# Where an instruction's semaphore waits stand: the last one at the instruction, the others at instructions ahead of it

## The chip, the core and the metric

The kernel runs on one core of a Trainium2 chip. The metric is the time of one execution in device microseconds. Five engines work side by side, each through its own instruction stream in a fixed order: TensorE (PE, matmuls; its weight loads are shown as PEld), VectorE (DVE), ScalarE (ACT), GpSimd (POOL) and SyncE (SP, which here only issues transfers). They meet at semaphores alone: an instruction adds one to a semaphore when it is done, and another engine's instruction waits until the count has reached a number.

## What is computed

Two kinds of layer alternate over a sequence of 2048 rows of 512 columns, twice each. Cut to what matters:

```python
x = x + A(layernorm(x)); x = x + B(layernorm(x))     # and both once more

def A(x):                                # 64 segments of 32 rows, one after the other
    mem = mem0                           # 8 rows
    for s in range(64):
        h = concat(mem, x[32 * s:32 * s + 32])          # 40 rows
        q, k, v = h @ Wq, h @ Wk, h @ Wv                # 32 heads of 128
        p = softmax(where(mask, q @ k.T / sqrt(128), -1e9))
        o = (p @ v) @ Wo
        mem, out[s] = o[:8], o[8:]       # the next segment needs mem

def B(x):                                # linear attention over all rows, 32 heads of 16
    pq, pk = phi(q), phi(k)              # phi(t) = (t + 1 if t > 0 else exp(t)) + 1e-6
    kv, z = pk.T @ v, pk.sum(rows)
    return (pq @ kv / (pq @ z + 1e-6)) @ wo
```

The 8 memory rows make layer A a recurrence: segment s + 1 can't begin its projections before segment s has ended its attention and its output projection, for those 8 rows.

## The kernel before

**The work.** `a_layer` (twice) goes over 64 segments. In each, `project` makes q, k and v from the 40 rows for two halves b = 0 and 1 of the heads (PE at L2159, and L2047 where loaded weights are used again). ACT or DVE move the results out of PSUM (`evac`, recorded at L1927 on ACT and L1928 on DVE), and DVE turns q and k (L2178). Then comes the path of the memory rows, for each half b in `mem_attention`: scores on PE (L2293, L2285), exponentials on ACT (L2300 for the memory rows, L2304 for the others), a product with a mask on DVE (L2308), P times V on PE (`pvm`, L2321), a reciprocal on DVE (L2326), scaling on ACT or DVE (L2336, L2338), a turn on DVE (L2328). `out_block` multiplies with Wo on PE (L2414), ACT takes over one half of the result (L1927) and DVE adds the other (L2425); `next_mem` puts the 8 new memory rows into place for the next segment (PE L2442, then L1927 or L1928). The attention of the 32 other rows (`x_attention`: PE L2364 and L2384, DVE L2352, L2371, L2374, L2391) and the pieces of layer B (`b_in`: L2597, L2668, L2675; `b_out`: L2059, L2831, L2843) aren't on that path; their matmuls stand between those of the path. Rows that are done go by transfers from SP and POOL (L1944) to a buffer, from which DVE adds them to x (L2491).

**The order.** Every operation is a node with a key, the engines that may run it, a planned cost and what it depends on. The order isn't found by the program: the table `PLACE` gives each node a place, a number from 1 to about 13500, and sometimes the engine. `schedule` sorts by it, hands out the 8 PSUM banks in that order and checks that whatever a node depends on stands ahead of it. Each engine gets its own nodes in that order. A node on PE is a group of 4 to 16 matmuls or so.

**The waits.** `finalize` (from L1718) gives each engine a semaphore and each sort of transfer one, and goes through the nodes in order. For a node it collects, for each semaphore, the highest count that the nodes it depends on will have reached, and leaves out what its engine knows already from earlier waits. What is left is `nd.waits`, with the highest count first:

```python
            items = sorted(need.items(), key=lambda kv: -kv[1])
...
            for si, v in items:
                if know[si] < v and infer[si] < v:
                    waits.append((si, v))
```

`emit` calls `wait_ge` (L1770) for each of them, in the order of the list, and then the node's first instruction. In the built program the wait that was called first is part of that instruction; the others stand ahead of it as instructions of their own, which the trace names EVENT_SEMAPHORE and puts at L1770. For a matmul with a weight load it is the load that carries the wait. As DVE's count runs ahead of ACT's, a PE node that waits for both engines has DVE's wait in its own instruction and ACT's in an EVENT_SEMAPHORE ahead of it. Of the 252 nodes at L2321, 159 wait for both: for DVE's product (L2308) and for ACT, which frees PSUM and moves v (L1927).

## Time and profile before

| | |
|---|---|
| median of 3 runs | 1542.52 us (1540.34 to 1544.87) |
| the profiled execution | 1539.86 us, its span 1538.1 us, so 1.8 us lie around the span |
| PE, DVE, ACT, POOL busy | 95%, 82%, 59%, 13% of the span |
| granted TensorE clock | 0.997 on average |

Three views are used below. The **page** gives totals and the chain of work that ended last, followed back from the end. The **timeline** lists instructions in the order of time: start in us, length in us, engine, line, what is written and read, how many were merged, and in brackets how long the engine had been idle before and who ended that. The view of **one source line** gives, for L1770, the semaphore instructions: how many, the shortest, median and longest record in ns, and when the first and the last began. A matmul's end is modelled, so starts are compared, not ends.

### The profile page before, as it was taken

The page shows a single profiled execution, that of the slowest core. Times are in us where ns is not written, and L with a number is a line of the kernel's source. Part 1 is how long each engine was busy: PE and PEld are TensorE (multiplying, and loading weights), DVE is VectorE, ACT ScalarE, POOL GpSimd, SP SyncE. Part 2 cuts the span into 40 slices and gives each one's busy share as a digit, 9 for nine tenths or more (in the row PEclk, how much of TensorE's full clock was granted, in tenths as well). Part 3 has the DMA queues.
Part 4 walks back from the last instruction along what each step waited for, and adds up shares of the span by engine and source line. Part 5 has one row for each costly group of instructions (what it writes and reads, how often), then busy time and mean ns, then how long its engine had stood idle before and what let it go on. Part 6 is the DMA issues. An engine that isn't in the chain of part 4 may idle for free.

```text
span 1538.1 us, 87084 instructions
## 1 busy us (share of the span) xinstructions
PE 1468.5 (95%) x42589; PEld 771.2 (50%) x36301; DVE 1268.3 (82%) x4106; ACT 904.9 (59%) x2630; POOL 199.7 (13%) x396
## 2 busy tenths in 40 slices
PE   7899999999999999999999999999999999999988
PEld 2445554545555545554544555455555455555444
DVE  4778888888888888888878888788888888887878
ACT  2555556555555665554555566666666666666656
POOL 3011110111111111111111110111111011111010
PEclk9999999999999999999999999999999999999999
DMA  9310100110100000001210101010101011011025
GB/s 390 97 31 23 34 14 19 27 24 24 23 20 10 24 23 24 24 23 34 59 24 22 24 19 26 23 28 23 28 17 23 23 27 27 24 24 32 16 44 136
DMA packets 81626, 60.04 MB, mean 39 GB/s; under 512 B 64040, under 2 KB 74600, under 8 KB 79720
## 3 DMA queue, kind: packets, MB, share of 16 engines
q1 hardware_dynamic: 67944, 37.58, 9.3%
q0 software_dynamic: 13152, 16.75, 3.8%
q8 instruction: 309, 5.06, 1.4%
q14 instruction: 61, 0.50, 0.1%
q10 hardware_dynamic: 160, 0.14, 0.0%
HBM read 25.57 MB, written 11.67 MB: 24 GB/s over the span
## 4 chain that ended last, share of the span: by engine, by line
PE 83%; DVE 7%; DMA 5%; ACT 4%; issue 1%; DVEq 0%; ACTq 0%
PE pb L2159 32%; PE pb L2047 19%; PE pb L2414 18%; PE pb L2059 2%; PE pb L2597 2%; PE pb L2321 2%; PE pb L2364 2%; ACT arena_sb L1927 2%; DMA dx_sb<-y_sb 2%; DMA arena_sb<-arena_sb 2%; PE pb L2384 1%; PE pb L2285 1%; PE pb L2442 1%; DMA Wk_sb<-in_A_Wk_dram 1%; DVE arena_sb L1928 1%
## 5 line engine op out<-in xcount | busy, mean ns | idle before, releaser
L1927 ACT ACTIVATE arena_sb<-pb 128x512 bf16<-128x512 f32 (+2 forms) x949 | 477.4, 532 | 259.2 <-PE pb L2047 142.5
L2159 PE MATMUL pb<-Wk_sb,arena_sb 128*32 128x512 bf16 x4192 | 362.9, 382 | 8.5 <-DMA Wk_sb<-in_A_Wk_dram 5.0
L2414 PE MATMUL pb<-Wo_sb,arena_sb 128*32 128x256 bf16 x10368 | 324.4, 273 | 9.2 <-DVE arena_sb L2326 4.9
L2178 DVE STREAM_TRANSPOSE arena_sb<-arena_sb 128x256 f32<-128x256 f32 x640 | 258.1, 425 | 39.7 <-ACT arena_sb L1927 34.3
L2414 PEld LDWEIGHTS pb<-Wo_sb,arena_sb 128*32 128x32 bf16 x10368 | 259.3, 97 | 60.3 <-DVE arena_sb L2326 33.5
L1944 POOL DMA_DIRECT2D dx_sb<-y_sb x246 | 125.3, 513 | 1052.9 <-DVE y_sb L2425 661.2
L2159 PE MATMUL pb<-Wq_sb,arena_sb 128*32 128x512 bf16 x3088 | 256.1, 379 | 0.9 <-DVE arena_sb L1928 0.5
L2159 PE MATMUL pb<-Wv_sb,arena_sb 128*32 128x512 bf16 x2560 | 252.3, 378 | 0.5 <-ACT arena_sb L1927 0.4
L2047 PE MATMUL pb<-Wv_sb,arena_sb 128*32 128x512 bf16 x2560 | 252.4, 378 | 0.0
L2159 PEld LDWEIGHTS pb<-Wk_sb,arena_sb 128*32 128x32 bf16 x4192 | 114.8, 97 | 218.6 <-issue 109.6
L2336 ACT ACTIVATE arena_sb<-pb,arena_sb 128x128 bf16<-128x128 f32 x525 | 160.7, 368 | 103.0 <-DVE arena_sb L2371 44.8
L2047 PE MATMUL pb<-Wq_sb,arena_sb 128*32 128x512 bf16 x2032 | 200.7, 380 | 0.0
L1928 DVE CAST arena_sb<-pb 128x512 bf16<-128x512 f32 (+2 forms) x315 | 157.7, 504 | 45.2 <-PE pb L2047 17.6
L2338 DVE TENSOR_TENSOR arena_sb<-pb,arena_sb 128x384 bf16<-128x384 f32 (+2 forms) x392 | 159.6, 408 | 9.9
L1927 ACT ACTIVATE outW_sb<-pb 64x256 f32<-64x256 f32 x150 | 56.7, 378 | 159.2 <-PE pb L2414 120.6
L2159 PEld LDWEIGHTS pb<-Wq_sb,arena_sb 128*32 128x32 bf16 x3088 | 84.4, 97 | 94.6 <-issue 35.7
L2352 DVE TENSOR_TENSOR arena_sb<-arena_sb,wx_sb 128x640 bf16<-128x640 bf16 x256 | 115.8, 470 | 0.9
L2159 PEld LDWEIGHTS pb<-Wv_sb,arena_sb 128*32 128x32 bf16 x2560 | 71.2, 96 | 88.0 <-issue 55.3
L2374 DVE STREAM_TRANSPOSE arena_sb<-arena_sb 128x192 f32<-128x192 f32 x256 | 92.7, 362 | 20.7 <-ACT arena_sb L2336 18.5
L2425 DVE TENSOR_TENSOR y_sb<-pb,outW_sb 64x256 bf16<-64x256 f32 x162 | 68.8, 424 | 47.2 <-ACT outW_sb L1927 44.2
L2364 PE MATMUL pb<-arena_sb 128*32 128x130 bf16 x3072 | 93.5, 220 | 1.1 <-issue 0.6
L2321 PE MATMUL pb<-arena_sb 128*32 128x130 bf16 x2016 | 74.5, 222 | 19.4 <-ACT arena_sb L2300 9.6
(128 smaller groups left out, 1803.2 us busy)
## 6 DMA issues: line engine op xcount, KB each, us to landing
Wk_sb<-in_A_Wk_dram SPq DMA_DIRECT2D x1, 4096.0 KB, 14.7
Wq_sb<-in_A_Wq_dram SPq DMA_DIRECT2D x1, 4096.0 KB, 24.1
Wv_sb<-in_A_Wv_dram SPq DMA_DIRECT2D x1, 4096.0 KB, 33.5
Wo_sb<-in_A_Wo_dram SPq DMA_DIRECT2D x8, 512.0 KB, 23.2
xs_scratch<-x_sb POOLq DMA_DIRECT2D x32, 128.0 KB, 2.0
pq_scratch<-arena_sb POOLq DMA_DIRECT2D x27, 128.0 KB, 2.2
x_sb<-xs_scratch POOLq DMA_DIRECT2D x16, 128.0 KB, 2.6
dx_sb<-y_sb SPq DMA_DIRECT2D x126, 12.0 KB
```

What stands on the lines that cost most here:

```text
L1927: return e.activation(o() if callable(o) else o, i() if callable(i) else i, ACTF.Copy)
L1928: return e.tensor_copy(o() if callable(o) else o, i() if callable(i) else i)
L1944: add(eng, lambda e: e.dma_start(o, i), 0.55 if eng == "pool" else 0.66, reads=reads, writes=writes, dsem="%s%d" % (kind, k), lat=lat + (0 ...
L2047: return pe.add_instruction(mybir.InstMatmult(name=nc.get_next_instruction_name(), engine=mybir.EngineType.PE, ins=[pe.lower_ap(x), pe.low ...
L2159: r = pe.matmul(o, blk[:, c, :], w, start=(c == 0), stop=(c == 3), tile_position=(0, 32 * j))
L2178: add("dve", lambda v: v.transpose(dst, src(img[:, k, :].bitcast(F32))), 0.445, reads=[("img", k, h) for h in range(2)], writes=[dkey])
L2321: r = pe.matmul(pv.f32()[32 * i:32 * i + 32, 0:130], w, m, start=start, stop=not start, skip_group_check=True, tile_position=(0, 32 * i))
L2336: x = e.activation(o[:, u, :], i()[:, u, :], ACTF.Copy, scale=r[:, u:u + 1])
L2338: return e.tensor_tensor(o, i(), r.unsqueeze(2).to_broadcast([128, n, 128]), ALU.mult)
L2352: add("dve", lambda v, b=b: v.tensor_tensor(Px[:, b, :].rearrange("p (n j x) -> p n j x", n=20, j=4), PQ[:, r2, b, 64:224].rearrange("p (n ...
L2364: r = pe.matmul(pv.f32()[32 * i:32 * i + 32, 130 * k:130 * k + 130], cols(b, k, i), vimg[:, r2, 4 * b + i, :], start=True, stop=True, skip ...
L2414: r = pe.matmul(tl.f32()[32 * j:32 * j + 32, 0:256], oT[:, b, f, n, :, :, e], Wo_sb[:, 16 * b + 4 * n + 2 * f + e, 256 * d:256 * d + 256], ...
```

## The change

At the end of `finalize`, once each node has its waits, a pass is added. `place` is a node's number in the order of all nodes. `source` estimates, in the same units, when a wait is met: for a transfer 60 places after the node that issues it, otherwise the producer's place plus 2 plus nine times its planned cost in us.

First, every list of two or more waits is sorted with the latest source first, so that this one becomes part of the instruction. Then, on ACT, PE and DVE, and not for the nodes of the setup, each further wait is tried at the nodes of the same engine ahead of this one, from the nearest back, up to 40 of them. If the source isn't before the place of the node that is looked at, the search ends and the wait stays where it was. If that node has no wait, it takes this one. On SP and POOL the lists are sorted and nothing is moved.

```diff
             nd.waits = waits
             nd.know = know
             last[nd.eng] = know
+        place = {nd: i for i, nd in enumerate(self.committed)}
+        source = {}
+        for nd in self.committed:
+            if nd.dsem is not None:
+                source[sidx[nd.dsem], nd.dval] = place[nd] + 60
+            elif nd.sig:
+                source[sidx[nd.eng], nd.val] = place[nd] + 2 + 9 * nd.cost[nd.eng]
+        for e in ENGINES:
+            mine = [nd for nd in self.committed if nd.eng == e]
+            for i, nd in enumerate(mine):
+                if len(nd.waits) < 2:
+                    continue
+                nd.waits.sort(key=lambda w: -source[w])
+                if e in ("sp", "pool") or nd.key[:2] < (0, 0):
+                    continue
+                left = nd.waits[:1]
+                for w in nd.waits[1:]:
+                    for o in reversed(mine[max(0, i - 40):i]):
+                        if source[w] >= place[o]:
+                            left.append(w)
+                            break
+                        if not o.waits:
+                            o.waits = [w]
+                            break
+                    else:
+                        left.append(w)
+                nd.waits = left
```

No instruction that computes or moves data is added, removed or reordered. Built, the program has 127 split-off waits on PE instead of 375, 108 on DVE instead of 208, and 35 on ACT instead of 49; on POOL and SP there are as many as before. 253 waits on PE, 187 on DVE and 14 on ACT stand at another instruction than before; on DVE 177 of these are waits for transfers, on PE 13.

## The prediction

> **What bounds the kernel now.** The page first: how full the engines are, and which engine holds the chain that ends last.

> ```profile
> span 1538.1 us, 87084 instructions
> ## 1 busy us (share of the span) xinstructions
> PE 1468.5 (95%) x42589; PEld 771.2 (50%) x36301; DVE 1268.3 (82%) x4106; ACT 904.9 (59%) x2630; POOL 199.7 (13%) x396
> ...
> PE 83%; DVE 7%; DMA 5%; ACT 4%; issue 1%; DVEq 0%; ACTq 0%
> ```

> PE bounds it, by its work and by the places where it stands still for ACT or DVE. A time saved on PE counts while the chain is on PE, 83% of the span. Then line L1770, the semaphore instructions, which are all that the change removes:

> ```profile
> L1770 PEldq EVENT_SEMAPHORE  x373: 51/51/473, 3.4 to 1526.0; - x187
> L1770 DVEq EVENT_SEMAPHORE  x206: 21/50/734, 24.4 to 1533.6; - x103
> L1770 ACTq EVENT_SEMAPHORE  x47: 17/17/17, 4.5 to 1477.4; - x47
> L1770 POOLq EVENT_SEMAPHORE  x26: 17/17/43, 16.8 to 1469.5; - x26
> ```

> A record of 51 ns on PE doesn't say what one costs. For that I took the timeline around two waits of PE. In the first, the wait that ends last is the split-off one:

> ```profile
> 802.76 0.29 DVE L2308 TENSOR_TENSOR arena_sb<-arena_sb 128x256 bf16<-128x256 bf16 x1 [0.20 <-ACT arena_sb L2300]
> ...
> 802.85 0.60 ACT L1927 ACTIVATE arena_sb<-pb 128x512 bf16<-128x512 f32 x1
> ...
> 803.56 0.15 PEld L2321 LDWEIGHTS pb<-arena_sb 128*32 128x32 bf16 x8 [0.71 <-DVE arena_sb L2308]
> 803.59 0.30 PE L2321 MATMUL pb<-arena_sb 128*32 128x130 bf16 x8 [0.22 <-ACT arena_sb L2300]
> ```
> ```profile
> L1770 PEldq EVENT_SEMAPHORE  x1: 51/51/51, 803.5 to 803.5; - x1
> ```

> DVE's product was done at 803.05, ACT's copy at 803.45. ACT's wait is the split-off one: its record begins at 803.5, and the matmul starts at 803.59, **0.14 us** after ACT's end. In the second, the split-off waits had passed and the instruction's own wait for DVE ends last:

> ```profile
> 793.59 0.24 DVE L2328 STREAM_TRANSPOSE arena_sb<-arena_sb 128x64 f32<-128x64 f32 x1
> ...
> 793.89 0.12 PEld L2414 LDWEIGHTS pb<-Wo_sb,arena_sb 128*32 128x32 bf16 x8 [0.35 <-DVE arena_sb L2328]
> 793.89 0.29 PE L2414 MATMUL pb<-Wo_sb,arena_sb 128*32 128x256 bf16 x4 [0.17 <-DVE arena_sb L2328]
> ```
> ```profile
> L1770 PEldq EVENT_SEMAPHORE  x2: 51/51/51, 793.3 to 793.5; - x2
> ```

> DVE ended at 793.83, the matmul starts at 793.89: **0.06 us**. So a last wait that sits in the instruction rather than ahead of it saves 0.08 us. And a split-off wait met in time costs nothing, as the matmul groups around one show:

> ```profile
> 243.80 0.39 PE L2159 MATMUL pb<-Wq_sb,arena_sb 128*32 128x512 bf16 x4
> 244.02 0.39 PE L2159 MATMUL pb<-Wk_sb,arena_sb 128*32 128x512 bf16 x4
> 244.24 0.39 PE L2159 MATMUL pb<-Wv_sb,arena_sb 128*32 128x512 bf16 x4
> 244.45 0.39 PE L2047 MATMUL pb<-Wv_sb,arena_sb 128*32 128x512 bf16 x4
> ```
> ```profile
> L1770 PEldq EVENT_SEMAPHORE  x2: 51/51/51, 243.8 to 244.9; - x2
> ```

> The group at 244.24 has a split-off wait ahead of it (the record at 243.8) and starts 0.22 after its neighbour, as the one at 244.02 without one does.

> **The change part by part.** (1) *The last wait moves into the instruction, on PE.* Comparing each split-off wait's producer with the start that PE could have had, I count 85 places where PE stood still for it, from the first row here to the last:

> ```profile
> 43.20 0.30 PE L2321 MATMUL pb<-arena_sb 128*32 128x130 bf16 x8 [0.18 <-ACT arena_sb L2300]
> ```
> ```profile
> 1484.11 0.30 PE L2321 MATMUL pb<-arena_sb 128*32 128x130 bf16 x8 [0.60 <-ACT arena_sb L2300]
> ```

> In 79 of them the late wait is no longer split off in the built program; the planned order of the two agrees with the trace. But they aren't all independent:

> ```profile
> 279.64 0.60 ACT L1927 ACTIVATE arena_sb<-pb 128x512 bf16<-128x512 f32 x1 [0.26 <-PE pb L2293]
> ...
> 280.24 0.60 ACT L1927 ACTIVATE arena_sb<-pb 128x512 bf16<-128x512 f32 x1
> ...
> 280.39 0.30 PE L2321 MATMUL pb<-arena_sb 128*32 128x130 bf16 x8 [0.65 <-ACT arena_sb L2300]
> ...
> 280.99 0.30 PE L2321 MATMUL pb<-arena_sb 128*32 128x130 bf16 x8
> ```

> The halves b = 0 and 1 of a segment wait for two copies that ACT makes one behind the other (ends 280.24 and 280.84). The second matmul starts 0.15 after the second copy, whenever the first one started; the pair gains 0.08 once. 17 places are such seconds, so 62 count: 62 x 0.08 = 5.0, of which 83% lie on the chain: **-4.1 us**. What is late next is the same wait, by 0.06 instead of 0.14; the other one had ended 0.4 us before (803.05 against 803.45).

> (2) *Moved waits, on PE.* 253 waits go to an earlier instruction that had none. PE takes its matmuls in order, so a moved wait that isn't yet met there holds that node and all behind it. By the trace of before 24 would hold, by 0.02 to 0.58 us, 3.3 together, at groups from the first row here to the last:

> ```profile
> 34.43 0.83 PE L2159 MATMUL pb<-Wq_sb,arena_sb 128*32 128x512 bf16 x12
> ```
> ```profile
> 1442.77 0.23 PE L2364 MATMUL pb<-arena_sb 128*32 128x130 bf16 x4
> ```

> Most stand at a matmul of the other rows:

> ```profile
> 852.54 0.60 ACT L1927 ACTIVATE arena_sb<-pb 128x512 bf16<-128x512 f32 x1
> ...
> 853.08 0.28 PE L2384 MATMUL pb<-arena_sb 128*32 128x130 bf16 x8
> ...
> 853.32 0.19 DVE L1928 CAST arena_sb<-pb 128x32 bf16<-128x32 f32 x1
> ```

> L2384 now waits for the copy that ends at 853.14 and starts at 853.20 instead of 853.08. Behind it PE waits for the DVE row that ends at 853.51 anyway: nothing lost. Three stand at `next_mem`, on the path of the memory rows:

> ```profile
> 1397.12 0.60 ACT L1927 ACTIVATE arena_sb<-pb 128x512 bf16<-128x512 f32 x1
> ...
> 1397.60 0.12 PEld L2442 LDWEIGHTS pb<-selm_sb,y_sb 128*32 128x32 bf16 x8
> 1397.60 0.22 PE L2442 MATMUL pb<-selm_sb,y_sb 128*32 128x16 bf16 x8
> ...
> 1397.90 0.19 DVE L1928 CAST arena_sb<-pb 128x32 bf16<-128x32 f32 x1
> ...
> 1398.15 0.10 PEld L2159 LDWEIGHTS pb<-Wk_sb,arena_sb 128*32 128x32 bf16 x4 [0.27 <-DVE arena_sb L1928]
> ```

> ACT ends at 1397.72, so L2442 starts at 1397.78 instead of 1397.60; L2059 is queued behind it, DVE's L1928 waits for it, and the next segment's L2159 for L1928. 0.18 at most, and 0.15 by the finer times of the trace: 3 x 0.15 = **+0.45**. Bounds for all moved waits: 0, if the 0.15 is made up, to +3.3. I take +0.45, as the rows show which ones sit on the path.

> (3) *DVE, ACT, POOL, SP.* On DVE 177 of 187 moved waits are for transfers; where they came from, the last one waited for is ACT's, or there is little idle time at all:

> ```profile
> L2425 DVE TENSOR_TENSOR y_sb<-pb,outW_sb 64x256 bf16<-64x256 f32 x162 | 68.8, 424 | 47.2 <-ACT outW_sb L1927 44.2
> ...
> L2491 DVE TENSOR_TENSOR x_sb<-x_sb,dx_sb 128x512 bf16<-128x512 bf16 (+1 forms) x32 | 12.6, 395 | 4.2 <-DMA dx_sb<-y_sb 3.9 <-issue 0.2
> ```

> At L2425 the wait for ACT is already the instruction's own: 0. At L2491 the last transfer's wait is split off in 18 of 32; at PE's 0.08 that is 1.4 at most, and the row bounds it at 4.2. I take 0, since DVE has only 7% of the chain. Every moved wait on DVE and ACT had been met by the trace, so none holds. On POOL and SP only the order within a list changes: 0, at most 26 x 17 ns = 0.4 either way.

> Sum: -4.1 + 0.45 = **-3.7 us**: 1536.2 for the profiled execution's 1539.86 (span 1538.1 and 1.8 around it). The median of the runs shown is 2.7 above that execution; against it the forecast is 1542.5 - 3.7 = **1538.8**.

> **The rivals.** *A, each split-off wait is worth its record.* If PE's sequencer lost 51 ns on each, blocked or not, 248 fewer would give 248 x 0.051 = 12.6: 1529.9. Against it: the group at 244.24, which loses nothing. For it: PE is 95% busy, and a shorter queue could show only where PE falls behind. [...]

> *B, the moved waits hold.* Place: PE's in-order queue, at the nodes that took a wait. 63 of the 253 were met less than 0.15 us before their new instruction starts, the 24 among them. If all 63 hold, at 0.14 each (3.3 / 24), that is 8.8, or 7.3 on the chain, and 7.3 - 4.1 = +3.2 remains: 1545.7. A held matmul of the memory path also delays the producers of the next moved waits; at twice the price it is +10.5: 1553. It decides once 35 of them (4.1 / 0.83 / 0.14) hold on the path; the trace has 3. [...]

> *C, the gain is swallowed.* PE comes 0.08 earlier to L2321 and waits so much longer at the next stop, because DVE (82% busy) sets the pace: 1542.5, give or take 2. For it: DVE's 82%; against it: the chain has 7% on DVE.

> That the change doesn't do what it says is excluded by the built program: 127 split-off waits instead of 375 on PE.

> **How the numbers follow.** A difference within 0.3%, 4.6 us here, is about what a measurement of this kernel can't tell from none. Forecast (-2 to -6): 0.48, of which 0.19 beyond -4.6. A (-6 to -13): 0.17. C: 0.19. B (+2 to +10): 0.16, of which 0.10 beyond +4.6. So faster 0.19 + 0.17 = 0.36, slower 0.10, the rest 0.54. The range leaves out the far half of A and what of B lies above +3.5: 1532 to 1546.

> **What would show it.** (1) L1770 on PE falls to about 125 records, and L2321 starts 0.06 after ACT's end where it now starts 0.14 after (803.59, 280.39); idle time ahead of L2321 falls by some 5 us. (2) L2442 near 1397.6 starts after the copy ahead of it; if many more L2364, L2384 or L2442 groups show new waits for ACT, B is right. (3) If idle time goes from L2321 to L2414 or L2442 instead of going, C is right. If PE's groups follow each other more closely where nothing waits, A is. A time above 1546 or below 1532 would prove the sum wrong.

## The result, and the profile after

| | before | after |
|---|---|---|
| median | 1541.14 us (1535.30 to 1546.67, 13 runs) | 1536.42 us (1531.46 to 1539.72, 13 runs) |
| profiled execution, its span | 1539.86, 1538.1 us | 1536.93, 1535.2 us |
| split-off waits recorded on PE | 373 | 125 |

The ratio is 0.9967 (95% interval 0.9952 to 0.9982), which is -5.1 us (-7.4 to -2.8). The forecast was -3.7. All lines from L1770 on stand 27 further down in the changed kernel: L2321 is L2348, L2414 is L2441, L2442 is L2469, L1927 is L1954.

First the page of the changed kernel, its totals:

```profile
span 1535.2 us, 86722 instructions
## 1 busy us (share of the span) xinstructions
PE 1468.6 (96%) x42589; PEld 765.3 (50%) x36301; DVE 1265.8 (82%) x4106; ACT 904.4 (59%) x2630; POOL 199.9 (13%) x396
```

PE is busy as long as before (1468.5 then). What fell is the time in which it stands: 1538.1 - 1468.5 = 69.6 us before, 66.6 now. The page's chain isn't used: after the change its shares add up to only half of the span.

Then the semaphore instructions, of the changed kernel, in the view of their line (count, shortest/median/longest in ns):

```profile
L1797 PEldq EVENT_SEMAPHORE  x125: 51/51/51, 3.4 to 1519.6; - x125
L1797 DVEq EVENT_SEMAPHORE  x106: 21/21/1115, 23.6 to 1498.2; - x106
```

On PE the longest record was 473 ns and is 51 now. The length of a record doesn't tell a late wait, though: the one ahead of 803.59 had 51 ns as well. The idle time is found in the groups by line, where the number behind the second bar is the time that PE stood ahead of the group. Before:

```profile
L2414 PE MATMUL pb<-Wo_sb,arena_sb 128*32 128x256 bf16 x10368 | 324.4, 273 | 9.2 <-DVE arena_sb L2326 4.9 <-issue 2.4 <-DVE arena_sb L2328 1.0
...
L2321 PE MATMUL pb<-arena_sb 128*32 128x130 bf16 x2016 | 74.5, 222 | 19.4 <-ACT arena_sb L2300 9.6 <-DVE arena_sb L2308 3.4 <-ACT arena_sb L1927 1.8
...
L2442 PE MATMUL pb<-selm_sb,y_sb 128*32 128x16 bf16 x1008 | 27.7, 175 | 6.9 <-DVE y_sb L2425 6.0 <-issue 0.2
```

After:

```profile
L2441 PE MATMUL pb<-Wo_sb,arena_sb 128*32 128x256 bf16 x10368 | 324.2, 273 | 8.6 <-DVE arena_sb L2353 5.6 <-issue 1.2 <-DVE arena_sb L2355 0.7
...
L2348 PE MATMUL pb<-arena_sb 128*32 128x130 bf16 x2016 | 73.7, 222 | 15.8 <-ACT arena_sb L1954 8.8 <-DVE arena_sb L2335 3.7 <-ACT arena_sb L2327 1.4
...
L2469 PE MATMUL pb<-selm_sb,y_sb 128*32 128x16 bf16 x1008 | 28.1, 175 | 6.5 <-DVE y_sb L2452 5.5 <-issue 0.2
```

The idle time ahead of P times V goes from 19.4 to 15.8. At the output projection and at `next_mem`, where rival C would have it reappear, it falls too, by 0.6 and 0.4. At the output projection this is "issue" (2.4 to 1.2), while the two waits for DVE went from 5.9 to 6.3 together, so little of the 3.6 came back there. The releaser named changes with it. The exponential (L2300) that was named before is one for which the group doesn't wait; in the place at 803.59 it ended at 803.56, between the end of the copy (803.45) and the late start:

```profile
803.34 0.22 ACT L2300 ACTIVATE arena_sb<-pb 128x64 bf16<-128x64 f32 x1
```

After the change the group has started before the next exponential ends, and ACT's copy (L1954), for which it does wait, is named. Now the place that the prediction showed at 803.59, in the timeline of the changed kernel:

```profile
801.00 0.29 DVE L2335 TENSOR_TENSOR arena_sb<-arena_sb 128x256 bf16<-128x256 bf16 x1 [0.20 <-ACT arena_sb L2327]
...
801.08 0.60 ACT L1954 ACTIVATE arena_sb<-pb 128x512 bf16<-128x512 f32 x1
...
801.73 0.30 PE L2348 MATMUL pb<-arena_sb 128*32 128x130 bf16 x8
```

DVE's product is done at 801.29, ACT's copy at 801.68, and the matmul starts at 801.73: 0.05 us after the copy, where it was 0.14. Over the whole trace, 80 groups at L2348 start 52 to 62 ns (median 53) after the producer of their last wait, and this wait is their own; 12 still start 144 to 147 ns after the producer of one that is split off. Before, 22 and 91 groups did (the latter 143 to 158 ns after). One of the twelve is the other place that the prediction named (280.39):

```profile
279.54 0.59 ACT L1954 ACTIVATE arena_sb<-pb 128x512 bf16<-128x512 f32 x1
...
279.98 0.28 DVE L2335 TENSOR_TENSOR arena_sb<-arena_sb 128x256 bf16<-128x256 bf16 x1
...
280.41 0.30 PE L2348 MATMUL pb<-arena_sb 128*32 128x130 bf16 x8 [0.43 <-ACT arena_sb L2327]
```

ACT's copy, planned last and now the group's own wait, ended at 280.13. DVE's product, now split off, ended at 280.26, and the matmul starts 0.15 after it. The sort goes by the plan; where the order on the chip differs from the plan by as little as the 0.13 us here, the late wait is the split-off one again.

### The profile page after: what moved, and what is told of

Read it like the earlier page. It is cut to its first block, busy times and chain, and to the rows that moved or that the text cites. A ratio compares the mean times of both kernels' runs of the same rounds, so it can differ in the third digit from the quotient of the medians.

```text
span 1535.2 us, 86722 instructions
## 1 busy us (share of the span) xinstructions
PE 1468.6 (96%) x42589; PEld 765.3 (50%) x36301; DVE 1265.8 (82%) x4106; ACT 904.4 (59%) x2630; POOL 199.9 (13%) x396
## 4 chain that ended last, share of the span: by engine, by line
PE 40%; DVE 4%; DMA 3%; ACT 2%; issue 1%; DVEq 0%
PE pb L2186 15%; PE pb L2074 9%; PE pb L2441 9%; PE pb L2086 2%; DMA arena_sb<-arena_sb 1%; DMA dx_sb<-y_sb 1%; PE pb L2391 1%; PE pb L2348 1%; PE pb L2624 1%; ACT arena_sb L1954 1%; PE pb L2411 1%; PE pb L2312 1%; PE pb L2469 1%; DVE arena_sb L1955 0%; DVE arena_sb L2205 0%
## 5 line engine op out<-in xcount | busy, mean ns | idle before, releaser
L1954 ACT ACTIVATE arena_sb<-pb 128x512 bf16<-128x512 f32 (+2 forms) x949 | 477.4, 532 | 256.8 <-PE pb L2074 141.6
L2186 PE MATMUL pb<-Wk_sb,arena_sb 128*32 128x512 bf16 x4192 | 359.0, 381 | 7.3 <-DMA Wk_sb<-in_A_Wk_dram 3.6
L2441 PE MATMUL pb<-Wo_sb,arena_sb 128*32 128x256 bf16 x10368 | 324.2, 273 | 8.6 <-DVE arena_sb L2353 5.6
L2441 PEld LDWEIGHTS pb<-Wo_sb,arena_sb 128*32 128x32 bf16 x10368 | 258.2, 97 | 61.1 <-DVE arena_sb L2353 34.9
L2074 PE MATMUL pb<-Wv_sb,arena_sb 128*32 128x512 bf16 x2560 | 249.9, 378 | 0.0
L2186 PE MATMUL pb<-Wv_sb,arena_sb 128*32 128x512 bf16 x2560 | 249.8, 378 | 0.0
L2186 PEld LDWEIGHTS pb<-Wk_sb,arena_sb 128*32 128x32 bf16 x4192 | 111.4, 97 | 218.5 <-issue 111.4
L1954 ACT ACTIVATE outW_sb<-pb 64x256 f32<-64x256 f32 x150 | 56.9, 379 | 157.6 <-PE pb L2441 120.5
L2452 DVE TENSOR_TENSOR y_sb<-pb,outW_sb 64x256 bf16<-64x256 f32 x162 | 68.7, 424 | 47.7 <-ACT outW_sb L1954 45.1
L2391 PE MATMUL pb<-arena_sb 128*32 128x130 bf16 x3072 | 93.4, 220 | 0.8 <-DVE arena_sb L2379 0.4
L2074 PE MATMUL pb<-Wk_sb,arena_sb 128*32 128x512 bf16 x928 | 91.6, 379 | 0.0
```

Of the source, the lines that this page charges most:

```text
L1954: return e.activation(o() if callable(o) else o, i() if callable(i) else i, ACTF.Copy)
L2074: return pe.add_instruction(mybir.InstMatmult(name=nc.get_next_instruction_name(), engine=mybir.EngineType.PE, ins=[pe.lower_ap(x), pe.low ...
L2186: r = pe.matmul(o, blk[:, c, :], w, start=(c == 0), stop=(c == 3), tile_position=(0, 32 * j))
L2391: r = pe.matmul(pv.f32()[32 * i:32 * i + 32, 130 * k:130 * k + 130], cols(b, k, i), vimg[:, r2, 4 * b + i, :], start=True, stop=True, skip ...
L2441: r = pe.matmul(tl.f32()[32 * j:32 * j + 32, 0:256], oT[:, b, f, n, :, :, e], Wo_sb[:, 16 * b + 4 * n + 2 * f + e, 256 * d:256 * d + 256], ...
```

## The experiments

My theory: a wait that ends last costs PE about 0.09 us more if it is split off, and nothing if it has been met; moved waits cost only where they hold the memory rows' path. The rivals were that every split-off wait costs its record (A), that moved waits cost wherever they hold PE (B), and that DVE swallows what PE gains (C). `source` and `place` below are those of the change. "Count" is the gain or loss that the trace of before gives for a program: at each place the start that the new waits would allow (145 ns after a split-off wait's producer, 54 after an own one), against the old one, nothing discounted. Differences are the ratio less 1, times the median of before in the same set (1539.4 to 1541.9 us).

**The sort alone, on all engines.** Edit: the changed kernel without the part that moves.

```diff
+                nd.waits.sort(key=lambda w: -source[w])
```

> Of the change, only the sorting: the wait planned last becomes part of the instruction, nothing moves to another instruction, and PE keeps all 375 split-off waits. By the trace of before, the places where PE stands still for a split-off wait fall from 85 to 11. Theory (what counts is where the last wait stands): 74 places less some 17 seconds of a pair, 57 x 0.08 us x 83% = -3.8 us, ratio 0.9975, and about as fast as the whole change. Rival A (each split-off wait costs its record): as many as before, so no gain, ratio 1.000. Rival B (moved waits hold PE): faster than the whole change by 0.5 us or more, since none is moved.

Measured: 0.9952 (0.9934 to 0.9970), -7.4 us. The sort alone is worth at least what the whole change is.

**The moves alone.** Edit: the changed kernel without the line above.

> Of the change, only the moving: the lists keep their old order, and the waits behind the first go to earlier instructions where the plan lets them. PE has 226 split-off waits instead of 375, but 82 of the 85 places where one is late stay, and 22 moved waits would hold an earlier matmul. Theory: no gain, +0.5 us at most from the held ones, ratio 1.000. Rival A: 149 fewer x 0.051 us = -7.6 us, ratio 0.995. Rival B: 22 held ones at 0.14 us, up to +2.6 us, ratio 1.002.

Measured: 1.0005 (0.9988 to 1.0021), +0.8 us. PE has 226 split-off waits instead of 375, and no time is gained. The group of P times V tells why, its idle time stays near 19.4:

```profile
L2347 PE MATMUL pb<-arena_sb 128*32 128x130 bf16 x2016 | 74.1, 222 | 18.4 <-ACT arena_sb L2326 9.5 <-DVE arena_sb L2334 3.2 <-DVE arena_sb L2352 1.4
```

**The sort on PE alone, on the other engines alone, and at P times V alone.** Edits: the loop of the first experiment over `("pe",)`, over `("pool", "sp", "act", "dve")`, and

```diff
+        for nd in self.committed:
+            if nd.eng == "pe" and nd.fn.__name__ == "pvm":
+                nd.waits.sort(key=lambda w: -source[w])
```

> Only the sorting, and on PE alone: ACT, DVE, POOL and SP keep their old lists, nothing moves. The places where PE stands still for a split-off wait fall from 85 to 11. The sorting on all engines gave 0.9952 where I had expected 0.9975. If all of that is PE's, this gives 0.995 again and the price of a late split-off wait on PE is about twice the 0.08 us x 83% I took; if the rest comes from the other engines, this gives 0.9975.

> Only the sorting, on all engines but PE; nothing moves. On DVE the late split-off waits fall from 21 to 3 (18 of them at L2491, the addition of the rows that came by transfer), on ACT from 4 to 1; on POOL 20 reloads of x have the wait for the transfer in the instruction instead of the one for DVE. As I had it in the prediction: 0, ratio 1.000. If the excess of the sorting comes from here: 0.9977 (-3.6 us).

> Of the changed kernel's pass only the sort, and only for the 252 nodes of pvm (L2321 of the kernel before); nothing is moved, all other lists stay. By the trace of before this takes away 78 places where PE stands for a wait that is split off, 6.0 us in all, of 7.0 us for the sort of all lists. My step (1), with the pairs taken once and the chain's share of PE: 6.0 / 7.0 x 4.1 = -3.5 us, a ratio of 0.9977. If every such place counts in full, with no discount for pairs and path: -6.0, 0.9961. If the gain of the sort doesn't come from these places, but from what the lists of other nodes do: within 1 us of no change, 0.9995 or more.

Measured, in this order: 0.9974 (0.9958 to 0.9991), -4.0 us; 1.0014 (0.9997 to 1.0030), no gain; 0.9976 (0.9959 to 0.9993), -3.7 us. The gain that shows is PE's, and most of it, if not all, comes from one kind of node. The third interval rules out that the gain comes from the lists of other nodes (0.9995 or more); it holds both -3.5 and -6.0. In the third, only these nodes' lists differ from before, nothing moves, there are as many split-off waits, and the idle time ahead of the group is that of the full change (15.8):

```profile
L2331 PE MATMUL pb<-arena_sb 128*32 128x130 bf16 x2016 | 74.3, 222 | 15.7 <-ACT arena_sb L1937 9.3 <-DVE arena_sb L2318 3.3 <-ACT arena_sb L2310 1.3
```

One thing stays open: PE alone and the other engines alone come to -4.0 and +2.2 us, which together is -1.8 (about 3.5 either way) and not the -7.4 (about 2.8 either way) of all engines at once. The expected 0.9977 for the other engines, which would have explained the rest, lies outside the measured interval. What the sort of all engines has beyond these two is not explained by any run here.

**The opposite order: the wait planned last is split off.** Edit, on all engines and then on PE alone:

```diff
+                nd.waits.sort(key=lambda w: source[w])
```

> The change turned round: the lists are sorted with the wait planned last at the end, so that it is split off, on all engines; nothing is moved. PE keeps 375 split-off waits; the places where one is late rise from 85 to 158. Theory: 73 x 0.08 us x 83% = +4.8 us, ratio 1.003. Rival A: no change, ratio 1.000. Rival C (a shift of 0.08 us on PE is swallowed, DVE sets the pace): no change on PE's account.

> The sorting turned round, on PE alone: late split-off waits on PE rise from 85 to 158, nothing else differs from before. On all engines this gave 1.0076; there 129 late split-off waits came up on DVE too, 90 of them at L2425 on the path of the memory rows. Theory (0.08 us each, 83% on the chain): +4.8 us, ratio 1.003, and the rest of the 1.0076 is DVE's. If PE's price is twice that: +9 us, ratio 1.006. Rival C: 1.000.

Measured: 1.0076 (1.0054 to 1.0099), +11.7 us, and 1.0046 (1.0029 to 1.0063), +7.1 us. The second is as the count has it (6.7), though its interval holds both ratios that I had written down, 1.003 and 1.006. The first expectation is a miss, since I had overlooked DVE: at 90 of the 162 sums of the output projection the split-off wait for ACT is the late one then. In the trace of the run on all engines 89 of these sums start 129 to 132 ns after ACT's end; before, where the wait is the sum's own, it is 33 ns (median). The groups of DVE by line, with 47.2 us of idle time in the kernel before; the first row is the experiment on all engines, the second that on PE alone:

```profile
L2438 DVE TENSOR_TENSOR y_sb<-pb,outW_sb 64x256 bf16<-64x256 f32 x162 | 68.8, 424 | 59.8 <-ACT outW_sb L1940 57.2
```

```profile
L2438 DVE TENSOR_TENSOR y_sb<-pb,outW_sb 64x256 bf16<-64x256 f32 x162 | 68.7, 424 | 49.4 <-ACT outW_sb L1940 46.3
```

So the order of the list matters on DVE as well, though the 4.6 us between the two runs are known only to about 4 either way. The kernel before had the order right at these sums already, so the sort had nothing to gain there.

**More split-off waits that have long been met.** Edit: each of PE's 1481 nodes with one wait gets a second one, for a count that POOL reaches at the start; listed last, it is split off.

```diff
+        for nd in self.committed:
+            if nd.eng == "pe" and len(nd.waits) == 1 and nd.key[:2] >= (0, 0):
+                nd.waits.append((sidx["pool"], 1))
```

> The kernel before with one more wait, listed last and so split off, at each of the 1481 nodes of PE that had a single wait. It is for a count of GpSimd that was reached in the setup, so it never holds. PE has 1856 split-off waits instead of 375, the late ones stay 85. Theory (a split-off wait that is met costs nothing): ratio 1.000, at most 1.002. Rival A: 1481 x 0.051 us = +75 us, ratio 1.049.

Measured: 1.0035 (1.0021 to 1.0049), +5.4 us for 1481 more, 3.6 ns each and more than the 1.002 expected at most. Not all of it need be a price of the waits: PE's idle time by "issue" (time in which it waits for nothing that the profile shows; more of it below) is 8.3 us in 14 stops in this trace, against 4.9 in 9 before and 2.8 to 6.1 in the kernels without added waits. The records of its line show what A would have charged at 51 ns each, 75 us:

```profile
L1773 PEldq EVENT_SEMAPHORE  x1854: 51/51/475, 3.4 to 1536.5; - x186
```

**A node's own wait split off.** Edit: the same with `insert(0, ...)` in place of `append(...)`, so that POOL's met wait takes the place in the instruction and the real one is split off; at all nodes with one wait, then only at those of the memory rows' attention, output projection and `next_mem` (`nd.key[2] in ("mem0", "mem1", "out", "next")`), then only at the rest.

> The kernel before with the wait of each of PE's 1481 single-wait nodes split off: the instruction itself has a wait that was met in the setup. The split-off waits are as many as in the run with met waits added (1856), but now they are the ones that end last: places where PE stands still for one rise from 85 to 515. Theory: 430 x 0.08 us x 83% = +29 us, ratio 1.019; counted at 1.0 on the chain +34 us. If the price is twice that: +57 us, ratio 1.037. Rival C: near the 1.0035 of the met waits.

> Like the kernel in which PE's own wait is split off at every node with one wait (+84 us), but only at the nodes of the memory rows' path (scores, P times V, output projection, next memory). By the trace of before 340 places start later, 25.5 us in all at 0.09 each; for all nodes the same count gave 39.1 us, and 84 were measured. If each late place costs about 2.15 times its count wherever it stands: +55 us, ratio 1.036. If what is beyond the count comes from this path alone, since a delay there is passed on to the other engines and back: +65 or more, 1.042 or more. If it comes from the other matmuls, which fall back because PE's stream is held up: +25, 1.016.

> The complement of the one before: the own wait is split off at PE nodes with one wait that aren't of the memory rows' attention, output projection or next memory (projections, the other rows' attention, layer B). By the trace of before 163 places start later, 13.7 us in all. At 2.15 times its count wherever it stands: +29 us, ratio 1.019. If the excess comes from the memory rows' path alone: +14 or less, 1.009 or less. If it comes from these nodes: +59, 1.038.

Measured: 1.0548 (1.0517 to 1.0580), +84 us; 1.0274 (1.0243 to 1.0305), +42 us; 1.0142 (1.0118 to 1.0166), +22 us. All are more than the counts of late starts (39.1, 25.5 and 13.7 us); the first is above everything expected, and the other two fit none of the readings that I had written down for them, since neither group of nodes is the only one at fault. The waits of PE in the first, summed by what ended them (us in total, times, longest), show what was missing in the count:

```profile
PE pb L2417 <- issue: 18.8, 27, 1.9
PE pb L2367 <- issue: 8.3, 9, 1.7
PE pb L2324 <- ACT arena_sb L2303: 8.1, 15, 0.7
```

"issue" is idle time in which PE waits for nothing that the profile shows. Over all rows of that view it is 4.9 us in 9 stops before, and 48.8 in 66, 22.9 in 35 and 10.4 in 16 in the three experiments. Count plus what "issue" grew by:

| split off | count | "issue" | sum | measured |
|---|---|---|---|---|
| all | 39.1 | 43.9 | 83.0 | 84 |
| memory rows' nodes | 25.5 | 18.0 | 43.5 | 42 |
| the rest | 13.7 | 5.5 | 19.2 | 22 |

The sum closes to within 3 us, with the "issue" of one trace for each kernel. What the stops are is told in the last section.

**More waits moved, with no margin.** Edit: the search may go back to the node right behind the producer; the sort keeps its margins. 51 split-off waits stay on PE, and by its own trace 67 groups are held by a moved wait, 11.7 us together; in the changed kernel it is 25 and 3.8.

```diff
             elif nd.sig:
+                met[sidx[nd.eng], nd.val] = place[nd]
                 source[sidx[nd.eng], nd.val] = place[nd] + 2 + 9 * nd.cost[nd.eng]
...
-                        if source[w] >= place[o]:
+                        if met[w] >= place[o]:
```

> The changed kernel, but a wait for another engine may be moved up to the node right behind its producer in the planned order (the 2 places and 9 places per us of margin are gone from the search; the sort keeps them). More waits are moved: 51 split-off waits stay on PE instead of 127. By the trace of before 68 moved places would hold PE, 11.1 us in all, against 27 and 3.3 us in the changed kernel by the same count. My step (2): only what holds on the memory rows' path counts, 0.45 of 3.3; then this kernel is about 1 us behind the changed one, 0.9975 where that one had 0.9967. Rival B: all that is held counts by the chain's share, 7.8 x 0.83 = +6.4 us behind the changed one, a ratio of about 1.001.

Measured: 1.0012 (0.9997 to 1.0028), +1.8 us, so 6.9 behind the changed kernel (about 3.3 either way; the two were run in different sets). That is rival B's price. One of the held groups, in its timeline:

```profile
837.59 0.59 ACT L1956 ACTIVATE arena_sb<-pb 128x512 bf16<-128x512 f32 x1
...
838.23 0.40 PE L2188 MATMUL pb<-Wq_sb,arena_sb 128*32 128x512 bf16 x4 [0.28 <-ACT arena_sb L1956]
...
838.67 0.23 PE L2350 MATMUL pb<-arena_sb 128*32 128x130 bf16 x4
```

L2188 needs nothing of this copy. It holds a wait that belongs to P times V behind it, starts 0.05 after the copy's end, and P times V (838.67) follows behind two groups of projection that could have run while PE stood.

## Why the prediction came out right, point by point

**Step (1), the late wait goes into the instruction: right, and the size within what can be measured.** The records fell to 125 as said, and the start after the producer from 0.14 to 0.05 (forecast 0.06). The idle time ahead of P times V fell by 3.6 us; I had said some 5. The sort alone on PE measured -4.0 (-6.5 to -1.4), on all engines -7.4 (-10.2 to -4.6); the forecast was -4.1. The count at full size is 85 x 0.08 = 6.8. So whether the two discounts were due (a pair counts once; only 83% lie on the chain) isn't settled: both sizes lie within or next to both intervals.

**Step (2), moved waits: the places right, the rule for their price not borne out.** I had forecast 24 held groups, 3.3 us together, three of them at `next_mem` at 0.15 each. The trace has 25, 3.8 us together, and three at L2469 with 0.14 each. The one that the prediction followed, in the timeline of the changed kernel:

```profile
1394.07 0.60 ACT L1954 ACTIVATE arena_sb<-pb 128x512 bf16<-128x512 f32 x1
...
1394.55 0.37 PE L2469 MATMUL pb<-selm_sb,y_sb 128*32 128x16 bf16 x8
...
1394.97 0.19 DVE L1955 CAST arena_sb<-pb 128x32 bf16<-128x32 f32 x1 [0.26 <-PE pb L2469]
...
1395.21 0.40 PE L2186 MATMUL pb<-Wk_sb,arena_sb 128*32 128x512 bf16 x4
```

The eight matmuls are two nodes. The first four start at 1394.55, the others, held for the copy that ends at 1394.67, at 1394.72. DVE's cast comes 0.42 after the first start (0.30 before), the next projection 0.66 after it (0.55 before): 0.11 are lost on the path. The other one followed, at a matmul of the other rows, is as forecast too:

```profile
851.35 0.60 ACT L1954 ACTIVATE arena_sb<-pb 128x512 bf16<-128x512 f32 x1
...
852.00 0.30 PE L2411 MATMUL pb<-arena_sb 128*32 128x130 bf16 x8
...
852.12 0.19 DVE L1955 CAST arena_sb<-pb 128x32 bf16<-128x32 f32 x1
...
852.37 0.40 PE L2186 MATMUL pb<-Wk_sb,arena_sb 128*32 128x512 bf16 x4
```

L2411 starts 0.05 after the copy (851.95), and the projection behind it starts 0.06 after the cast's end (852.31), for which it had to wait anyway. What failed is the step from here to all the others: the sum took only the three at `next_mem`, "on the path of the memory rows", and so +0.45. Where 7.9 us more were held (11.7 against 3.8), 6.9 more were measured, so held time does count for the most part, also at the projections, where I gave it no price. For the changed kernel itself this would be up to +3 instead of +0.45, but its 25 places can't be priced from here: -5.1 stands against -4.0 and -7.4 for the sort alone. And 0.9 of its 3.8 us are a single group near the start (35.31), held for the transfer of Wv, for which the group behind it had to wait before the change as well (35.67 then, 35.54 now); that hold cost nothing.

The two doubts have opposite signs. With the full count in both steps the sum would have been -6.8 + 3.3 = -3.5, with the discounts in both it is -3.7; the measurement can't tell these apart, and that the total fits doesn't show that the discounts were right.

**Step (3), the other engines: right.** Their sort alone gives no gain, and DVE's sums wait as long after (47.7 us) as before (47.2):

```profile
L2452 DVE TENSOR_TENSOR y_sb<-pb,outW_sb 64x256 bf16<-64x256 f32 x162 | 68.7, 424 | 47.7 <-ACT outW_sb L1954 45.1
```

**The rivals.** A falls: 3.6 ns for a split-off wait that has been met, not 51, and removing 149 of them by the moves alone brought nothing. So next to nothing of a record of 51 ns is lost as long as the wait is met. Where PE stands for that very wait, the start comes 146 ns after the producer's end instead of 53. C falls by the measured gain, and by the rows of L2441 and L2469: the waits for DVE there are 6.3 and 5.5 us after and 5.9 and 6.0 before, so the 3.6 didn't move to them. B has the mechanism (838.23: PE idle for 0.28 us, for a wait that the group there doesn't need) and, by the last experiment, the price, but not the number in the changed kernel: 25 holds, where I had 35 as the point from which it decides. With 67, not all of them on that path, the gain is gone, at +1.8.

No version run here beats the sort alone. The sort alone and the changed kernel can't be told apart (0.9934 to 0.9970 against 0.9952 to 0.9982); that the moves cost something in the changed kernel is likely from the experiment with more of them, but not shown.

## What to carry to other kernels

Where an instruction waits for several engines, look in the trace for which wait ends last, and list that one first: in this kernel it is worth 0.09 us on PE at each place where the engine stands for it, and next to nothing where it doesn't. Counting split-off waits says little: 1481 more of them that had been met cost 5 us, and 73 more late ones cost 7. On PE a wait moved to where it wasn't met yet held groups that don't need it as well (two of projection at 838.23, with PE idle for 0.28 us). Without a margin behind the producer 67 groups were held, by 11.7 us together; with the margin it was 25 groups and 3.8 us, and that kernel was 6.9 us faster.

## What the runs showed of the hardware that was not expected

PE's program is loaded while it runs, and in the kernels with own waits split off PE's stops by "issue" go with these loads. The page of the kernel in which all own waits are split off has them as a DMA queue of their own (packets, MB, share):

```profile
q8 instruction: 315, 5.16, 1.4%
```

```profile
630.62 0.24 PE L2367 MATMUL pb<-arena_sb 128*32 128x130 bf16 x3
631.21 0.47 PE L2367 MATMUL pb<-arena_sb 128*32 128x130 bf16 x20 [0.35 <-issue]
```

Three matmuls of a group start, then nothing for 0.35 us, then the others, in a group whose own list of waits is that of before. The kernel before has about as many loads, but only 9 stops and 4.9 us of "issue" in all, and the changed one 6 stops and 3.9 us; where all own waits are split off it is 66 stops and 48.8 us. Why split-off waits bring the loads to light is open: no run here separates it.
